# Transposing normed activation blocks by DMA instead of by TensorE in a four-layer kernel

## The chip, the cores and the metric

The kernel runs on one core of a Trainium2 chip; the rounds of the experiments ran on different chips, so a ratio always compares runs of the same rounds. The metric is the time of one execution on the device in microseconds (us), the median of several runs. All runs quoted here of one kernel agree within 0.2%. A profile covers a span about 1.8 us shorter than the timed execution (1694.7 against 1696.5 us), so times from profiles are only compared with times from profiles.

Names: PE is TensorE's matmul row, PEld its weight loads, DVE is VectorE, ACT is ScalarE, POOL is GpSimd, SP is SyncE. A "q" after a name (SPq, ACTq) means that engine's instruction queue. PSUM is the memory that TensorE writes to. An evacuation is the pass that takes a result out of PSUM.

## The reference

Four layers on x, 2048 rows of 1024 features in bfloat16. Layers 1 and 3 are linear attention, layers 2 and 4 a gated feed-forward block; each reads a layer norm of x and adds to x.

```python
x = A_x
x = x + _A_ref(_layernorm(x), A_wqkv, A_wo)                    # linear attention, 32 heads of 32
x = x + _B_ref(_layernorm(x), B_W_gate, B_W_up, B_W_down)      # relu(gate) * up, 3584 wide
x = x + _A_ref(_layernorm(x), A_wqkv, A_wo)
x = x + _B_ref(_layernorm(x), B_W_gate, B_W_up, B_W_down)
# _A_ref: phi(t) = where(t > 0, t + 1, exp(t)) + 1e-6; kv = sum phi(k) v; z = sum phi(k)
#         o = phi(q) kv / (phi(q) z + 1e-6); return o @ wo
```

## The kernel before

x lies in memory as 16 blocks of 128 rows. Four blocks make a quarter. A matmul needs the normed block with features on the partitions, so each block is normed on VectorE (statistics, then one pass that writes `xn`) and then transposed. Each of the 4 layers norms and transposes 16 blocks, 64 in all. `xn` has two buffers.

```python
self.xio = pool("xio", 3)      # x as loaded
self.xnp = pool("xnp", 2)      # xn
self.ps = pool("ps", 4, space=PSUM)
...
def ln_norm(self, layer, t):
    src = self.xin.pop(t) if layer == 0 else self.x[t]
    ...                                            # 2 x bn_stats, bn_aggr on VectorE
    nc.scalar.activation(out=rstd, in_=mv[:, 1:2], func=ACT.Ln, bias=self.eps5[:, 0:1])
    nc.scalar.activation(out=rstd, in_=rstd, func=ACT.Exp, scale=-0.5)
    xn = self.xnp.tile([P, D], BF16, tag="xn")
    nc.vector.tensor_scalar(out=xn, in0=src, scalar1=mv[:, 0:1], scalar2=rstd[:, 0:1], ...)
    if layer == 0:
        nc.gpsimd.tensor_copy(out=self.x[t], in_=src)
        if t + 3 < self.ST:
            self.load_x(t + 3)                     # a DMA on ScalarE's queue
    return xn

def ln_turn(self, layer, t, xn):
    ...
    tp = self.pst.tile([P, self.KT, P], BF16, tag="tr")
    for kt in range(self.KT):                      # 8 transposes of 128 x 128
        nc.tensor.transpose(tp[:, kt, :], xn[:, kt * P:(kt + 1) * P], self.ident)
    ...                                            # PSUM to xnT, VectorE and ScalarE in turn

def ln_later(self, layer, q, first, step, lag):    # norm and transpose between matmul groups
    for j in range(QT):
        ...
        self.later.at(first + j * step, norm)      # the transpose follows `lag` groups later
```

In an attention layer, the first stage makes K and V for four quarters of 16 groups of 8 matmuls. K goes through `phi` (an exponential on ScalarE, two passes on VectorE); V is copied out of PSUM by ScalarE; the `kv` matmuls follow. The later part, which I call the attention tail, makes Q, a denominator matmul per 128 features, and the output, which VectorE adds to x.

The tile framework's scheduler decides the order of instructions on each engine. The order of the program is a priority, not a promise. Weights (1 MB tiles, a ring of seven) are loaded from SyncE's queue.

## Time and profile before

Time 1696.49 us, median of 3 runs (1696.45 to 1697.39).

| what | number | where read |
|---|---|---|
| PE busy | 1675.2 of 1694.7 us | page, part 1 |
| share of PE in the chain that ended last | 95% | page, part 4 |
| 32 matmuls of 512 columns | 6.91 us, 216 ns each | chain in order of time |
| eight transposes between full matmuls | 0.45 us | chain in order of time |
| DMA engines busy in layers 2 and 4 | 45 to 49%, 37% in the last quarter | table of stretches |

From the page of the kernel before: the span, the busy time, and the chain that ended last, by engine and by line.

```profile
span 1694.7 us, 19592 instructions
PE 1675.2 (99%) x8304; PEld 778.6 (46%) x8304; DVE 595.0 (35%) x1002; ACT 392.5 (23%) x723; POOL 21.2 (1%) x54
q1 hardware_dynamic: 191488, 192.95, 35.4%
PE 95%; DVE 3%; ACT 1%; DMA 1%; issue 0%; DVEq 0%; ACTq 0%
PE acc L380 23%; PE pg L363 23%; PE pu L363 23%; PE ps L229 13%; PE ps L298 5%; PE ps L311 5%; PE tp L153 2%; PE kv L204 1%; PE ps L269 1%; DMA xin<-in_A_x_dram 1%; DVE stats L130 1%; DVE x L315 0%; DVE xn L137 0%; DVE pq L273 0%; ACT r L271 0%
```

TensorE is the bound, and the transposes ("PE tp L153") are 2% of the chain. The next lines are the chain in order of time (start, duration, what), in the first layer of the kernel before.

```profile
21.21 4.32 PE ps L229 x20
25.52 0.45 PE tp L153 x8
25.97 6.91 PE ps L229 x32
32.88 0.45 PE tp L153 x8
33.32 6.91 PE ps L229 x32
```

Full matmuls run back to back, and eight transposes cost 0.45 us of the stream, 56 ns each. The matmul record of one transpose says 219 ns, but successive ones overlap. The price of a transpose is read from the spacing.

VectorE's groups, by shape (line, engine, operation, shapes, count, busy us, mean ns, idle time before and its releaser), show what one block's norm costs: two statistics of 691 ns and one pass of 807 ns.

```profile
L130 DVE BATCH_NORM_STATS2 stats<-x 128x6 f32<-128x512 f32 x96 | 65.4, 691 | 2.4
L315 DVE TENSOR_TENSOR x<-x,ps 128x512 f32<-128x512 f32 x64 | 43.2, 675 | 12.5 <-PE ps L311 12.0
L137 DVE TENSOR_SCALAR xn<-x,mv,rstd 128x1024 bf16<-128x1024 f32 x48 | 38.7, 807 | 16.1 <-PE tp L153 15.9
```

The last line also shows that `xn` waited 15.9 us in sum for the PE transposes: the buffers of `xn` were freed by TensorE.

### The profile page before, as it was taken

How to read it: one execution, taken by the hardware profiler on the slowest of the kernel's cores; microseconds unless marked ns; L12 is line 12 of the kernel's file. 1: busy time of each engine (PE TensorE's matmuls, PEld its weight loads, DVE VectorE, ACT ScalarE, POOL GpSimd, SP SyncE). 2: the span in 40 equal slices, each digit the busy share in tenths (PEclk: the TensorE clock that was granted, in tenths of full speed). 3: DMA queues.
4: the chain of work that ended last, by engine and by line, in shares of the span. 5: the costliest groups of instructions: out<-in, count | busy, mean ns of one | idle time of the engine just before them, and what ended most of it. 6: DMA issues, size and time to landing. Idle time of an engine off the chain costs nothing.

```text
span 1694.7 us, 19592 instructions
## 1 busy us (share of the span) xinstructions
PE 1675.2 (99%) x8304; PEld 778.6 (46%) x8304; DVE 595.0 (35%) x1002; ACT 392.5 (23%) x723; POOL 21.2 (1%) x54
## 2 busy tenths in 40 slices
PE   6999999999999999999999999999999999999999
PEld 3554444444444444444455544444444444444444
DVE  7445994312321231232144279832112202211211
ACT  3436641210220120022033374412002101100110
POOL 3100000000000000000000000000000000000000
PEclk9999999999999999999999999999999999999999
DMA  7103011455445444444510220134554464455441
GB/s 242 32 26 125 0 51 52 145 157 169 149 134 164 151 142 156 149 149 134 182 58 1 71 80 1 50 100 140 165 182 145 130 196 135 140 180 177 146 144 34
DMA packets 198489, 202.60 MB, mean 120 GB/s; under 512 B 3840, under 2 KB 196352, under 8 KB 198400
## 3 DMA queue, kind: packets, MB, share of 16 engines
q1 hardware_dynamic: 191488, 192.95, 35.4%
q10 hardware_dynamic: 6912, 8.39, 1.5%
q8 instruction: 65, 1.06, 0.3%
q14 instruction: 24, 0.20, 0.0%
HBM read 197.13 MB, written 4.19 MB: 119 GB/s over the span
## 4 chain that ended last, share of the span: by engine, by line
PE 95%; DVE 3%; ACT 1%; DMA 1%; issue 0%; DVEq 0%; ACTq 0%
PE acc L380 23%; PE pg L363 23%; PE pu L363 23%; PE ps L229 13%; PE ps L298 5%; PE ps L311 5%; PE tp L153 2%; PE kv L204 1%; PE ps L269 1%; DMA xin<-in_A_x_dram 1%; DVE stats L130 1%; DVE x L315 0%; DVE xn L137 0%; DVE pq L273 0%; ACT r L271 0%
## 5 line engine op out<-in xcount | busy, mean ns | idle before, releaser
L363 PEld LDWEIGHTS <-t 128*128 128x128 bf16 x3584 | 349.5, 98 | 416.3
L363 PE MATMUL pg<-xnT,t 128*128 128x512 bf16 x1792 | 423.3, 379 | 0.0
L363 PE MATMUL pu<-xnT,t 128*128 128x512 bf16 x1792 | 423.3, 379 | 0.0
L380 PE MATMUL acc<-t,hT 128*128 128x512 bf16 x1792 | 388.1, 379 | 0.0
L369 DVE TENSOR_TENSOR hT<-pu,rg 128x512 bf16<-128x512 f32 x224 | 154.9, 692 | 586.0 <-PE pu L363 586.0
L368 ACT ACTIVATE rg<-pg 128x512 f32<-128x512 f32 x224 | 133.3, 595 | 891.5 <-PE pg L363 891.4
L380 PEld LDWEIGHTS <-hT 128*128 128x128 bf16 x1792 | 175.3, 98 | 211.4
L229 PE MATMUL ps<-t,xnT 128*128 128x512 bf16 x1024 | 230.4, 380 | 0.0
L229 PEld LDWEIGHTS <-xnT 128*128 128x128 bf16 x1024 | 98.5, 98 | 109.9 <-issue 1.1
L298 PE MATMUL ps<-xnT,t 128*128 128x512 bf16 x512 | 121.6, 379 | 0.2
L311 PE MATMUL ps<-T,pq 128*128 128x512 bf16 x512 | 113.4, 379 | 0.0
L174 ACT ACTIVATE e<-ps 128x512 f32<-128x512 f32 x128 | 76.2, 595 | 137.1 <-PE ps L229 116.4
L391 DVE TENSOR_TENSOR xo<-x,acc 128x512 bf16<-128x512 f32 x32 | 22.0, 688 | 171.1 <-PE acc L380 167.5
L388 DVE TENSOR_TENSOR x<-x,acc 128x512 f32<-128x512 f32 x32 | 22.0, 688 | 159.4 <-PE acc L380 157.9
L311 PEld LDWEIGHTS <-pq 128*128 128x128 bf16 x512 | 50.0, 98 | 58.5
L298 PEld LDWEIGHTS <-t 128*128 128x128 bf16 x512 | 49.7, 98 | 56.1 <-issue 1.7
L175 DVE TENSOR_SCALAR e<-e 128x512 f32<-128x512 f32 x128 | 54.9, 429 | 57.3 <-ACT e L174 56.3
L130 DVE BATCH_NORM_STATS2 stats<-x 128x6 f32<-128x512 f32 x96 | 65.4, 691 | 2.4
L153 PE MATMUL tp<-ident,xn 128*128 128x128 bf16 x512 | 39.8, 222 | 14.3 <-DVE ident L109 11.6
L235 ACT ACTIVATE pkv<-ps 128x512 bf16<-128x512 f32 x64 | 38.2, 597 | 66.2 <-PE ps L229 66.2
L153 PEld LDWEIGHTS <-xn 128*128 128x128 bf16 x512 | 34.7, 99 | 29.5 <-DVE xn L137 12.0
L315 DVE TENSOR_TENSOR x<-x,ps 128x512 f32<-128x512 f32 x64 | 43.2, 675 | 12.5 <-PE ps L311 12.0
(41 smaller groups left out, 517.8 us busy)
## 6 DMA issues: line engine op xcount, KB each, us to landing
t<-in_B_W_gate_dram SPq DMA_DIRECT2D x56, 1024.0 KB, 5.4
t<-in_B_W_up_dram SPq DMA_DIRECT2D x56, 1024.0 KB, 5.2
t<-in_B_W_down_dram SPq DMA_DIRECT2D x64, 896.0 KB, 5.8
t<-in_A_wqkv_dram SPq DMA_DIRECT2D x12, 1024.0 KB, 5.6
xin<-in_A_x_dram ACTq DMA_DIRECT2D x16, 256.0 KB, 3.6
t<-in_A_wo_dram SPq DMA_DIRECT2D x4, 1024.0 KB, 5.2
out_dram<-xo ACTq DMA_DIRECT2D x32, 128.0 KB, 3.0
```

The costliest lines, as they stand in the source:

```text
L130: nc.vector.bn_stats(out=stats[:, c, :], in_=src[:, c * fmax:(c + 1) * fmax])
L153: nc.tensor.transpose(tp[:, kt, :], xn[:, kt * P:(kt + 1) * P], self.ident)
L174: nc.scalar.activation(out=e, in_=ps, func=ACT.Exp)
L175: nc.vector.tensor_scalar(out=e, in0=e, scalar1=1.0, scalar2=1e-6, op0=ALU.min, op1=ALU.add)
L229: nc.tensor.matmul(ps, lhsT=self.xnT[l, q][:, kt, j * P:(j + 1) * P], rhs=w[:, kt, :], start=(kt == 0), stop=(kt == KT - 1))
L298: nc.tensor.matmul(ps, lhsT=w[:, kt, (g % 4) * P:(g % 4 + 1) * P], rhs=self.xnT[l, sc][:, kt, :], start=(kt == 0), stop=(kt == KT - 1))
L311: nc.tensor.matmul(ps, lhsT=pq[sc, g // 4][:, g % 4, j * P:(j + 1) * P], rhs=T[g // 2][:, g % 2, n2 * NW:(n2 + 1) * NW], start=(g == 0), s ...
L315: nc.vector.tensor_tensor(out=xs, in0=xs, in1=ps, op=ALU.add)
L363: nc.tensor.matmul(ps, lhsT=w[:, kt, fi * P:(fi + 1) * P], rhs=self.xnT[l, q][:, kt, :], start=(kt == 0), stop=(kt == KT - 1))
L368: nc.scalar.activation(out=rg, in_=pg, func=ACT.Relu)
L369: nc.vector.tensor_tensor(out=h[:, fi, :], in0=pu, in1=rg, op=ALU.mult)
L380: nc.tensor.matmul(acc[j], lhsT=hT[ft // 4][:, ft % 4, j * P:(j + 1) * P], rhs=wd[:, k, :], start=(ft == 0), stop=(ft == self.FT - 1))
```

## The change

Intent: take the transposes off the engine that bounds the kernel, and their copies off VectorE and ScalarE. All but the first four blocks (the first quarter of the first layer) are transposed by a DMA on SyncE's queue, straight from `xn` to `xnT`.

```diff
+        dst = self.xnT[layer, q][:, :, j * P:(j + 1) * P]
+        if layer or q:
+            nc.sync.dma_start_transpose(out=dst, in_=xn)
+            return
         tp = self.pst.tile([P, self.KT, P], BF16, tag="tr")
         for kt in range(self.KT):
             nc.tensor.transpose(tp[:, kt, :], xn[:, kt * P:(kt + 1) * P], self.ident)
-        dst = self.xnT[layer, q][:, :, j * P:(j + 1) * P]
         self.n_evac += 1
```

Four lines are added above the transposes and one is taken out below them, so L153 of before is L157 of after, L229 is L232, L235 is L238. L153 of after is the DMA transpose.

## The prediction

> **What bounds the kernel now.** TensorE. The page shows PE busy 1675.2 of 1694.7 us at a granted clock of 1.0, and the chain of waits that ended last is 95% PE. In that chain 32 matmuls of 512 columns take 6.91 us (216 ns each), back to back, for almost the whole span. In the stretches table a quarter of the second and fourth layers (146.8 us) has PE busy throughout. What is not PE lies in the first 21 us (x loads, statistics) and in the attention layers' tails, where VectorE is on the chain (180 to 195 us).
>
> **What the change removes.** 60 of 64 blocks lose 8 PE transposes (480 matmuls and weight loads), and 30 VectorE copies (683 ns) plus 30 ScalarE copies (1,023 ns). The matmul record says 219 ns, but that is latency: between full matmuls the chain shows eight transposes costing 0.45 us ("PE tp L153 x8, 0.45", after 20 matmuls that end at 25.52 and before those that begin at 25.97). 60 x 0.45 = 27 us on TensorE, nearly all on the critical path (the chain gives that line 1.6%, 27 us). The copies, 20.5 us of VectorE and 30.7 us of ScalarE, are mostly off it: worth about zero.
>
> **What it adds.** 60 DMA transposes of 256 KB on the SyncE queue, 15.7 MB beside 202.6. No transpose is in this trace. The Trainium skill, "DMA: Bandwidth & Descriptors", section "Latency and other measured facts", gives 261 GB/s for a DMA transpose, so about 1 us of data; with the 3.6 us that a 256 KB x load takes to land in this trace I estimate 3.5 to 4.5 us from issue to landing, 1.2 to 2 us of the queue. DMA is about 45 to 49% busy in the second and fourth layers, idle in most of the attention layers: bandwidth is no limit.
>
> **What it moves.** The instruction order shows the scheduler hoisting the norms. (a) xn has two buffers, and each is now released by a landed transpose instead of by PE, so VectorE, in order, waits at the norm of block t for the transpose of t-2. (b) In the first layer all norms of blocks 4 to 15 now stand before the first exponential-feature work of the second quarter. The first transpose queues behind seven 1 MB weight loads, the last of which lands at 28.7 us; from there five pairs at about 4.7 us end near 54 us, where TensorE needs its first PSUM buffer back at about 55 us. I expect 0 to 8 us of PE stall there. (c) In the tail of each attention layer a block now costs VectorE about 3.75 us (two adds 0.675, two statistics 0.69, aggregate 0.2, norm 0.81) against 3.46 us of PE: some 3 us behind, absorbed by four PSUM buffers. (d) Weight loads behind a waiting transpose lose nothing: the ring is 7 tiles, 48 us, ahead.
>
> **Sum.** 1696.5 - 27 + about 3 = 1672 us, range 1666 to 1688. Faster than 2% (under 1662.6) would need 34 us, more than is removed.
>
> **What would show it.** PE 480 instructions fewer; a quarter of the second layer 145.0 instead of 146.8 us, no wait in it; one PE gap, near 50 to 60 us, released by VectorE, whose norms wait on transposes; median landing 3.5 to 4.5 us; the third layer 5 to 7 us shorter.
>
> **What would make it wrong.** Landing of 8 us or more: the first layer's ten norms, two at a time, would stall PE by some 20 to 35 us and the attention tails too, eating all the gain. Or transposes that hold up weight loads on the same rings. Or no stall at all: 1668.

## The result, and the profile after

After: 1679.53 us, median of 4 runs (1679.36 to 1679.69); before, of the same rounds, 1696.82 us. The ratio is 0.9898, 95% interval 0.9881 to 0.9915. The kernel gained 17 us of the 27 us that left TensorE.

The same lines of the page of after:

```profile
span 1677.8 us, 18805 instructions
PE 1651.6 (98%) x7824; PEld 752.0 (45%) x7824; DVE 572.4 (34%) x972; ACT 365.3 (22%) x693; POOL 20.9 (1%) x54
q1 hardware_dynamic: 254848, 208.69, 42.0%
PE 91%; DVE 5%; ACT 2%; DMA 2%; issue 1%; DVEq 0%; ACTq 0%
xnT<-xn SPq DMA_TRANSPOSE x60, 3.1
```

480 matmuls are gone, and PE's share of the chain fell from 95% to 91%: TensorE now waits for something. The last line is from the list of DMA issues: 60 transposes, 3.1 us median from issue to landing.

Where the gain went is seen by cutting the span at the first matmul of each stage. Starts are read from the timeline of PE; the durations are differences of starts, in us, and layer 4 ends with the span. "Due" is 0.45 us times the transposes that left the stage.

| stage | before | after | gained | due |
|---|---|---|---|---|
| layer 1, start to the first Q matmul | 141.41 | 141.82 | -0.41 | 5.4 |
| layer 1, attention tail | 127.05 | 127.18 | -0.13 | 1.8 |
| layer 2 | 587.30 | 580.16 | 7.14 | 7.2 |
| layer 3, K and V stage | 122.94 | 117.58 | 5.36 | 5.4 |
| layer 3, attention tail | 127.05 | 127.16 | -0.11 | 1.8 |
| layer 4 | 588.95 | 583.90 | 5.05 | 5.4 |

Layers 2 and 4 and the third layer's K and V stage gained what was due. Three stages gained nothing: 5.8 us are missing in the first, 1.9 in each tail.

**The first layer.** The timeline of PE in after (start, us, engine, line, operation, count, and in brackets the idle time and what ended it):

```profile
31.68 12.39 PE L232 MATMUL ps<-t,xnT 128*128 128x512 bf16 x56 [0.36 <-DVE pkv L179]
43.90 0.40 PE L207 MATMUL kv<-pkv 128*128 128x129 bf16 x4
46.93 0.40 PE L207 MATMUL kv<-pkv 128*128 128x129 bf16 x4 [2.63 <-ACT pkv L238]
47.16 2.63 PE L232 MATMUL ps<-t,xnT 128*128 128x512 bf16 x8
49.59 1.07 PE L207 MATMUL kv<-pkv 128*128 128x129 bf16 x8
```

TensorE waited 2.63 us for a copy of V by ScalarE (L238). Then it ran slowly: from 48.1 to 51.6 us the granted clock was 0.51, and matmuls of 512 columns started up to 427 ns apart instead of 216. Summed from the starts of matmuls, from 21.65 us to the end of the stage, the holes (0.5, 0.2 and 2.8 us) and the slow stretch (1.7 us) make about 5 us; the steady run of matmuls also began 0.6 us later than in before (21.65 against 21.04). So this wait cost more than its own length. e3 below, with the same wait, has the same slow stretch; e5 and e8, with single waits of up to 1.76 us, have none; in e9 it follows only the second of two waits of 3.2 us. No run here tests what sets it. (Half speed for 3.5 of 1678 us is 0.1%: it is what an average clock of 0.999 hides.) The timeline of ACT shows why the copy was late:

```profile
40.83 0.34 ACTq L184 DMA_DIRECT2D xin<-in_A_x_dram  x1
41.21 0.60 ACT L238 ACTIVATE pkv<-ps 128x512 bf16<-128x512 f32 x1 [2.52 <-DVE xn L137]
42.09 0.29 ACT L134 ACTIVATE rstd<-mv,eps 128x1 f32<-128x1 f32 x1 [0.28 <-DVE mv L132]
```

```profile
45.86 0.29 ACT L134 ACTIVATE rstd<-mv,eps 128x1 f32<-128x1 f32 x1 [0.86 <-DVE mv L132]
46.19 0.20 ACT L135 ACTIVATE rstd<-rstd 128x1 f32<-128x1 f32 x1
46.30 0.58 ACT L238 ACTIVATE pkv<-ps 128x512 bf16<-128x512 f32 x1
```

V copies stand in one row with x loads, which wait for a norm to free their buffer ("DVE xn L137", 2.52 us before the copy at 41.21), and with `rstd` steps, which wait for VectorE's statistics. The copy that TensorE waited for is the one at 46.30; it stands behind an `rstd` step that waited 0.86 us. The instruction order of VectorE says what happened: in before, 10 norms stood ahead of the first `phi` work of the second quarter; in after all 16 do. Once no TensorE instruction stood between norm and norm, the scheduler put them earlier. (Both orders are read from the traces; why the scheduler chose so is not recorded.) VectorE got through them only at 57 us, shown by its timeline in after:

```profile
56.84 0.55 DVE L137 TENSOR_SCALAR xn<-xin,mv,rstd 128x1024 bf16<-128x1024 bf16 x1 [0.60 <-ACT rstd L135]
57.32 0.43 DVE L178 TENSOR_SCALAR e<-e 128x512 f32<-128x512 f32 x1
```

**The tails.** VectorE in the first attention tail of before, at the change from output to Q matmuls:

```profile
195.72 0.43 DVE L175 TENSOR_SCALAR e<-e 128x512 f32<-128x512 f32 x1 [0.85 <-ACT e L174]
196.18 0.69 DVE L176 SCALAR_TENSOR_TENSOR pq<-ps,e 128x512 bf16<-128x512 f32 x1
```

The same place in after, VectorE and then PE:

```profile
193.01 0.81 DVE L137 TENSOR_SCALAR xn<-x,mv,rstd 128x1024 bf16<-128x1024 f32 x1
196.83 0.43 DVE L178 TENSOR_SCALAR e<-e 128x512 f32<-128x512 f32 x1 [0.85 <-ACT e L177]
197.17 0.81 DVE L137 TENSOR_SCALAR xn<-x,mv,rstd 128x1024 bf16<-128x1024 f32 x1
197.90 0.68 DVE L179 SCALAR_TENSOR_TENSOR pq<-ps,e 128x512 bf16<-128x512 f32 x1
```

```profile
198.64 0.39 PE L272 MATMUL ps<-pq,zrep 128*128 128x512 bf16 x1 [0.73 <-DVE pq L179]
```

Two norm passes of 0.81 us more have come into this stretch, one of them between the two halves of `phi`. `pq` starts 1.7 us later than in before (0.4 us of it because the tail itself began later), and the denominator matmul that needs it finds TensorE idle for 0.73 us. Before, the third norm stood later, at 204.24 us. Another such gap, of 0.78 us, stands at 229.54 us. In the whole tail 14 norm passes run in after, 6 in before. The holes between the starts of its matmuls sum to 5.3 us in after and 3.4 in before, which is the 1.9 us that are missing.

### The profile page after: what moved, and what is told of

Read it like the earlier page. It is cut to its first block, busy times and chain, and to the rows that moved or that the text cites. A ratio compares the mean times of both kernels' runs of the same rounds, so it can differ in the third digit from the quotient of the medians.

```text
span 1677.8 us, 18805 instructions
## 1 busy us (share of the span) xinstructions
PE 1651.6 (98%) x7824; PEld 752.0 (45%) x7824; DVE 572.4 (34%) x972; ACT 365.3 (22%) x693; POOL 20.9 (1%) x54
## 4 chain that ended last, share of the span: by engine, by line
PE 91%; DVE 5%; ACT 2%; DMA 2%; issue 1%; DVEq 0%; ACTq 0%
PE acc L383 23%; PE pu L366 23%; PE pg L366 23%; PE ps L232 12%; PE ps L301 5%; PE ps L314 3%; DVE stats L130 2%; DMA xin<-in_A_x_dram 1%; DVE xn L137 1%; PE kv L207 1%; PE ps L272 1%; DVE x L318 1%; DVE pq L276 0%; DMA xnT<-xn 0%; ACT r L274 0%
## 5 line engine op out<-in xcount | busy, mean ns | idle before, releaser
L232 PE MATMUL ps<-t,xnT 128*128 128x512 bf16 x1024 | 229.1, 382 | 0.4 <-DVE pkv L179 0.4
L232 PEld LDWEIGHTS <-xnT 128*128 128x128 bf16 x1024 | 99.5, 98 | 115.5 <-issue 3.3
L134 ACT ACTIVATE rstd<-mv,eps 128x1 f32<-128x1 f32 x64 | 18.8, 295 | 321.0 <-DVE mv L132 320.8
L238 ACT ACTIVATE pkv<-ps 128x512 bf16<-128x512 f32 x64 | 38.3, 598 | 75.2 <-PE ps L232 70.2
L276 DVE TENSOR_TENSOR pq<-pq,r 128x512 bf16<-128x512 bf16 x64 | 43.8, 689 | 7.9 <-ACT r L275 5.3
L274 ACT ACTIVATE r<-ps,eps 128x512 f32<-128x512 f32 x64 | 43.4, 686 | 9.0 <-PE ps L272 8.3
```

What stands on the lines that cost most here:

```text
L232: nc.tensor.matmul(ps, lhsT=self.xnT[l, q][:, kt, j * P:(j + 1) * P], rhs=w[:, kt, :], start=(kt == 0), stop=(kt == KT - 1))
L274: nc.scalar.activation(out=r, in_=ps, func=ACT.Ln, bias=self.eps6[:, 0:1])
L276: nc.vector.tensor_tensor(out=p, in0=p, in1=r, op=ALU.mult)
```

## The experiments

Theories at this point:

- Order: the 10 us are lost because the norms stand earlier in VectorE's order (and their `rstd` steps and x loads in ScalarE's).
- Landing: they are lost because a norm waits for landed transposes (transposes whose data have arrived) through two `xn` buffers, wherever it stands.
- Contention: the transposes' traffic slows other transfers.

The stage times of every run, from its profile, as in the table above (K/V is layer 1 from the start to its first Q matmul):

| run | time, us | K/V of layer 1 | tail 1 | tail 3 |
|---|---|---|---|---|
| before | 1696.5 | 141.41 | 127.05 | 127.05 |
| after | 1679.5 | 141.82 | 127.18 | 127.16 |
| e1_pin_all | 1670.4 | 135.91 | 125.44 | 125.42 |
| e2_pin_l0 | 1673.8 | 135.79 | 127.16 | 127.16 |
| e3_pin_rest | 1675.9 | 141.62 | 125.43 | 125.44 |
| e4_l0_pe | 1679.1 | 141.35 | 127.19 | 127.19 |
| e5_xnp3 | 1679.4 | 141.06 | 127.15 | 127.15 |
| e6_xio4 | 1681.6 | 143.75 | 127.16 | 127.16 |
| e7_double | 1687.6 | 147.66 | 128.66 | 128.01 |
| e8_pin_double | 1672.6 | 138.71 | 125.42 | 125.43 |
| e9_xl_pool | 1688.3 | 149.39 | 127.20 | 127.19 |
| e10_pin_before | 1701.3 | 144.17 | 127.16 | 127.17 |
| e11_xn_act | 1676.6 | 141.72 | 125.78 | 125.78 |
| e12_pin_pool | 1672.9 | 138.48 | 125.43 | 125.44 |

The start of the first layer varies by some tenths of a us between profiles with the first x loads, so differences under 1 us in the K/V column are not read. All twelve kernels of the experiments gave correct results.

### e1, e2, e3: the norms held in their places

The edit to the kernel after. `issue_after` orders instructions on one engine without a wait for data: a norm may not be issued before the evacuation that stands ahead of it in the program.

```diff
+    def pinned(self, layer, t):
+        if self.dve is not None:                  # e2: and layer == 0;  e3: and layer
+            return self.tc.issue_after(self.dve.ins)
+        return nullcontext()
...
             def norm(t=t):
-                xn = self.ln_norm(layer, t)
+                with self.pinned(layer, t):
+                    xn = self.ln_norm(layer, t)
...
-        nc.vector.scalar_tensor_tensor(out=out, in0=ps, scalar=0.0, in1=e,
+        self.dve = nc.vector.scalar_tensor_tensor(out=out, in0=ps, scalar=0.0, in1=e,
...   # the same for the other five VectorE passes that read PSUM or follow a denominator
```

> Every later norm is kept behind the VectorE evacuation that stands before it in the program; transposes stay on DMA. After: 1679.5 us. Order theory (the 10 us missing from the 27 are lost because the norms stand earlier in VectorE's order: 5.8 in the first layer's key/value stage, 1.9 in each attention tail): all comes back, 1669 to 1671. Landing theory (norms wait for landed transposes through two xn buffers wherever they stand): no change, 1678 to 1681, or slower, because data now lands nearer to its use. Contention theory (DMA traffic slows something): no change.

> The same pin for the first layer's norms alone. Order theory: the key/value stage of the first layer ends 5 to 6 us sooner (about 136.5 instead of 142.0 us), total 1674, tails as after. Landing theory: 1679 to 1680.

> The same pin for all norms but those of the first layer. Order theory: each of the two attention tails gives back 1.5 to 2 us (the two TensorE gaps of 0.73 and 0.78 us before a denominator matmul go), total 1675 to 1676; first stage as after. Landing or contention theory: 1679 to 1680.

Measured: e1 1670.37 us (1670.23 to 1670.89), ratio to before 0.9844 (0.9827 to 0.986). e2 1673.84 us, ratio 0.9864 (0.9849 to 0.9879). e3 1675.93 us, ratio 0.9876 (0.9861 to 0.9891). The pin in the first layer took 6.0 us off its stage and touched nothing else; the pin in the rest took 1.7 us off each tail and touched nothing else. With both, the gain over before is 26.3 us of the 27 in the profiles. In e1, 8 norms stand ahead of the second quarter's first `phi` work, and 4 norm passes run in each tail. The chain in order of time of e1, in the first layer, has no hole left:

```profile
20.86 21.80 PE ps L239 x101
42.66 0.47 PE kv L214 x8
43.13 1.73 PE ps L239 x8
44.86 0.47 PE kv L214 x8
```

The order theory gave every number, and landing and contention did not. In e1 the transposes even land later in the median. 28 of the 60 are now issued in layers 2 and 4, beside weight loads, against 17 in after; those 28 land in 7.0 to 9.6 us:

```profile
L154 SPq DMA_TRANSPOSE xnT<-xn x60: 1231/1238/5024, 27.5 to 1430.5; - x60
DMA to landing us min/median/max: 3.0/4.5/9.6
```

The same lines of after (instruction time in the queue in ns, minimum, median and maximum, then the landing time):

```profile
L153 SPq DMA_TRANSPOSE xnT<-xn x60: 1231/1233/2136, 24.5 to 1098.8; - x60
DMA to landing us min/median/max: 3.0/3.1/6.8
```

So the faster kernel has the slower transposes. What counts is where the norms stand. e1 is also the version that beats both kernels.

### e4: the first layer's transposes back on TensorE

```diff
-        if layer or q:
+        if layer:
```

> All 16 transposes of the first layer on TensorE again, the other 48 by DMA. If the whole loss of 5.8 us sits in the first layer and nothing else hangs on it: 5.8 back, 12 x 0.45 = 5.4 lost, 1679 +- 1, that is, the twelve DMA transposes of the first layer bring nothing as scheduled. If the loss has another place: 1685.

Measured: 1679.10 us, ratio to before 0.9896 (0.9881 to 0.991), as expected. The twelve DMA transposes of the first layer, as scheduled in after, brought nothing; the stage takes 141.35 us with them on TensorE and 141.82 by DMA.

### e5, e6: one buffer more

```diff
-        self.xnp = pool("xnp", 2)
+        self.xnp = pool("xnp", 3)       # e5 (a fourth does not fit)
```

```diff
-        self.xio = pool("xio", 3)
+        self.xio = pool("xio", 4)       # e6; load_x(t + 4), four loads at the start
```

> After, with three xn buffers instead of two (all that the memory leaves room for); 15 instead of 16 norms stand before the second quarter's first exponential-feature work. If landed transposes pace the row of norms through the xn buffers, a third of that wait goes and the first layer's key/value stage ends 2 to 4 us sooner (142.0 us in after), total 1675 to 1678. If x loads or the order alone pace it: 1679 to 1680. The tails, where VectorE's work counts and not the buffers, stay or get worse (a norm more can stand early).

> After, with four x load buffers instead of three, each load asked for one block earlier. If the x loads (4.4 us to land, their issue held in ScalarE's queue until a norm has freed the buffer) pace the row of norms: first stage 2 to 4 us shorter, total 1675 to 1678. If landed transposes or the order alone pace it: 1679 to 1680.

Measured: e5 1679.42 us, ratio 0.9901 (0.9886 to 0.9916), no change from after. e6 1681.59 us, ratio 0.9912 (0.9897 to 0.9927), outside both expectations: a little slower, its stage 1.9 us longer. In e6 TensorE's longest wait for a V copy is 3.62 us instead of 2.63; why is not tested. One buffer more in either ring alone did not shorten the row of norms. Both together were not tried: by the expectation of e5 three `xn` buffers are all that the memory leaves room for. (In the trace of e5, 16 norms stand before the second quarter's first `phi` work and not 15 as expected; in that of e9, 15 and not 14.)

### e7, e8: every DMA transpose twice

```diff
             nc.sync.dma_start_transpose(out=dst, in_=xn)
+            nc.sync.dma_start_transpose(out=dst, in_=xn)
```

> After, with every DMA transpose issued twice to the same place (the same result). DMA traffic of the transposes and the time until an xn buffer is free go up by 1.2 to 2 us each. Landing theory for the first layer as scheduled in after: its stage gets 3 to 8 us longer, total 1683 to 1688. If transposes' duration is off the path everywhere: 1679 to 1681. The scheduler puts 13 norms instead of 16 before the second quarter here, which works the other way.

> The kernel with all norms pinned (1670.4 us), every DMA transpose issued twice. Order theory: with the norms in their places the transposes' time and traffic are hidden, 1670 to 1672. Landing or contention theory: 5 us or more slower, 1675 and up.

Measured: e7 1687.64 us, 8.1 us over after: 5.8 in the first stage, 1.5 and 0.9 in the tails, nothing in the rest. e8 1672.57 us, 2.2 us over e1, all of it in the first stage (2.8 us in the profile), nothing in the tails. The upper end of what was expected for e8 was 1672, so it was a near miss, but the 2.2 us are clear of noise (1672.28 to 1673.02 against 1670.23 to 1670.89). The trace of e8 shows where they come from: in the first stage norms wait three times, 10.0 us in all and 3.81 at most, for landed transposes, which they never do in e1; V copies stand behind these norms' steps and x loads in ScalarE's queue; and TensorE waits 1.42 and 1.18 us for two V copies. So in the first stage the transposes' time matters with the norms in place too, once it is doubled. Whether it is the landing or the traffic, these two runs do not separate there. Of the 60 more transposes, 22 in e7 and 28 in e8 are issued in layers 2 and 4, and these cost nothing, so contention for DMA is excluded there.

### e9, e12: x loads from GpSimd's queue

```diff
-        self.nc.scalar.dma_start(out=xin, in_=self.x_v[:, t, :])
+        self.nc.gpsimd.dma_start(out=xin, in_=self.x_v[:, t, :])     # e9: after; e12: e1
```

> After, with the x loads issued from GpSimd's queue instead of ScalarE's. In after TensorE waits at 44 us for a copy of V on ScalarE, which stands behind an x load in ScalarE's queue, which waits for a norm to free its buffer. If that queue is the bridge by which late norms reach TensorE: the wait of TensorE on the V copies goes and the first layer's stage ends 3 us or more sooner (142.0 us in after), total 1674 to 1677. If VectorE's own order is the bridge (the second quarter's exponential-feature work stands behind all norms): 1679 to 1681. 14 norms instead of 16 stand before the second quarter here.

> The kernel with all norms pinned (1670.4 us) and the x loads on GpSimd's queue. Order theory: nothing is left to gain there, 1669.5 to 1671. If ScalarE's queue still holds something up: under 1669.

Measured: e9 1688.25 us, ratio 0.9953 (0.9936 to 0.9969), slower than after, outside both expectations. e12 1672.92 us, slower than e1 by 2.6 us. In both, TensorE's steady run of matmuls begins later (24.29 and 23.91 us, against 21.65 in after and 20.70 in e1): the first x blocks came later. That is enough for e12, which has no other wait in its stage. In e9 TensorE also still waits for V copies, 3.24 and 3.20 us, although no x load stands in ScalarE's queue. The timeline of ACT in e9:

```profile
48.59 0.29 ACT L134 ACTIVATE rstd<-mv,eps 128x1 f32<-128x1 f32 x1 [3.92 <-DVE mv L132]
48.91 0.20 ACT L135 ACTIVATE rstd<-rstd 128x1 f32<-128x1 f32 x1
49.02 1.07 ACT L238 ACTIVATE pkv<-ps 128x512 bf16<-128x512 f32 x2
54.86 0.29 ACT L134 ACTIVATE rstd<-mv,eps 128x1 f32<-128x1 f32 x1 [4.77 <-DVE mv L132]
```

The V copies stand behind the norms' own `rstd` steps, which wait for VectorE. So an x load in ScalarE's queue is not needed for the wait; the `rstd` steps suffice. How much the x loads add in after this run does not show, since its own x blocks came later.

### e10: the pin on the kernel before

The edit of e1, on the kernel with TensorE transposes.

> Control: the pin on the old kernel, transposes on TensorE. If the pin is worth something by itself, it is faster than 1696.5 us; the order theory says the old kernel's transposes, TensorE instructions in program order, held the norms in place already: 1695 to 1698.

Measured: 1701.30 us, ratio 1.0029 (1.0014 to 1.0044): slower by 5 us, where I expected no change. Both K and V stages got longer (2.8 us in the first, 1.8 in the third layer); in the profile TensorE's transposes in the first layer now wait for norms held back (six waits before "DVE xn", 2.2 us in all), and in the third layer six transposes start 0.27 to 0.35 us late, 1.7 us in all. Here the pin puts norms later than before had them: 8 instead of 10 ahead of the second quarter's first `phi` work, 4 instead of 6 in each tail. The pin is no gain by itself. With transposes on TensorE an early norm is worth having, because TensorE stops at a transpose whose block is not ready. With transposes by DMA, e1 shows that it is not.

### e11: the norm pass of layers 2 to 4 on ScalarE

```diff
-        nc.vector.tensor_scalar(out=xn, in0=src, scalar1=mv[:, 0:1], scalar2=rstd[:, 0:1], ...)
+        nc.vector.tensor_scalar(out=nmr, in0=mv[:, 0:1], scalar1=rstd[:, 0:1], scalar2=-1.0,
+                                op0=ALU.mult, op1=ALU.mult)
+        nc.scalar.activation(out=xn, in_=src, func=ACT.Identity, bias=nmr[:, 0:1],
+                             scale=rstd[:, 0:1])       # layer 1 as it was
```

> After, with the normalizing pass of layers 2 to 4 on ScalarE instead of VectorE (0.81 us a block off VectorE, about 1 us on ScalarE). If VectorE's load in the attention tails is what makes the denominators' input late: each tail gives back 1 to 2 us, total 1675.5 to 1678. If it is when the norms stand and not on which engine, since ScalarE too is in the denominator's chain: 1679 to 1681.

Measured: 1676.56 us, ratio 0.9883 (0.9868 to 0.9898). Each tail gave back 1.4 us with the norms still early. So in the tails it is VectorE's load that counts for most of the loss: 0.81 us a block at a time when VectorE is the engine that TensorE waits for. Moving the pass to another engine or to another time cures it nearly alike (125.78 and 125.44 us).

## Why the prediction was right or wrong

The time, 1679.5 us, lies in the stated range (1666 to 1688), and the gain stayed under 2%, as said. The point, 1672, was 7.5 us too low, and the range was wide: it allowed for new waits of up to 18 us. Point by point:

- **What bounds the kernel, and what the change removes.** Right. 0.45 us a block, 27 us in all: the stages without a new wait gained 7.14 of 7.2, 5.36 of 5.4 and 5.05 of 5.4 us, and e1 gained 26.3 us in the profile.
- **What it adds.** The estimate of 3.5 to 4.5 us to landing was too high for after (3.1 us), and 1.2 to 2 us of the queue held at its low end (1.23 us). Bandwidth was no limit, as predicted; e7 and e8 show it in layers 2 and 4.
- **(b), the first layer.** The stall was foreseen within 0 to 8 us; the sum took about 3 for everything, and 5.8 us were measured here. The end of the row of norms was predicted near 54 us and was 57 us. The place was wrong: the gap was announced near 50 to 60 us, released by VectorE; it began at 44 us and was released by ScalarE. I followed VectorE's order to its end and did not ask what the same norms put into ScalarE's order, nor did I count the slow stretch after the gap. That the size fell within 0 to 8 us is partly luck.
- **(c), the attention tails.** This step failed. The prediction counted 3.75 us of VectorE a block against 3.46 of TensorE and said the lag would be "absorbed by four PSUM buffers". Those buffers can absorb late adds; they did not help the next step, whose denominator matmul waits for `pq`, which VectorE writes after the same queue of work. Measured 1.9 us in each tail, 3.8 in all; e3 gives 3.5 of it back and e11 2.8.
- **(d), weight loads.** Right: nothing was lost in layers 2 and 4.
- **The quarter of the second layer.** Predicted 145.0 us; two successive starts of the chain's long piece of down matmuls in after are 510.89 and 655.93, 145.04 us apart. The third layer was predicted 5 to 7 us shorter and is 5.25.
- **"No stall at all: 1668".** e1 is that case nearly: 1670.4 us.

In sum: the prediction counted 3 us of new waits, and there were about 10 (5.8 and twice 1.9, and some tenths in layer 4). Shown by the runs: the norms' place in the order causes all but about 1 us of it (e1 to e3), VectorE's load makes most of the loss in the tails (e11), and doubled transposes lengthen the first stage, with the norms early (e7) and in their places (e8). Open: how the pace of the row of norms divides between landing transposes, arriving x loads and statistics, and what sets the slow stretch after TensorE's wait. One buffer more of either kind did not shorten the stage.

## What to carry to other kernels

When an instruction on the bounding engine goes, ask what it was holding in place. Here the transposes cost 27 us, and as TensorE instructions between norm and norm they also kept 22 norms (6 in the first stage, 8 in each tail) from crowding in front of more urgent work; the scheduler used its new freedom and gave 10 us back until one ordering edge took it away. Compare the order on every engine that the moved work touches, the small steps on ScalarE too, and count where an engine off the critical path sits directly before the bound one.

## What the Trainium skill lacked or had wrong

- "Advanced Engine Details and Errata", section "X-Bar Transpose (TRN2)", says that transpose DMAs are as fast as regular ones, and "DMA: Bandwidth & Descriptors", section "Latency and other measured facts", gives 261 GB/s where a middle dimension is not contiguous, as in `xnT` here. Here, from 183 to 197 us of after, three transposes and no weight load moved 56 GB/s at a DMA share of 0.30, that is 187 GB/s of busy time; the weight loads of before moved 192.95 MB in 35.4% of 1694.7 us, 322 GB/s of busy time. Both are worked out from the profile's busy shares.
- "VectorE: DVE Perf Modes", section "The three transpose paths", gives 390 ns for a 128x128 transpose on TensorE and 1309 ns by DMA. A pipelined TensorE transpose cost 56 ns of the stream, and one DMA of eight such tiles 1.23 us of the queue and 3.1 us to landing. The table has one time for each path and none in a stream, which is what the choice between the paths needs. (The spacing of successive matmuls stands on another page, not beside the table.)
- No page gives the time of a DMA transpose beside weight loads: in layer 2 of e1 (262 to 420 us) the four transposes of the stretch held SyncE's queue 2.4 to 5.0 us and landed in 7.5 to 8.5 us, against 1.23 and 3.1 us in quiet stretches.
